# One head of each of two batches changes its layout, and five queues get a new order: fused clustered attention and gated MLP

## The chip, the cores and the metric

One core of a Trainium2 chip. The metric is the device time of one execution of the kernel in microseconds; the median of several runs counts. The profiled execution is one more run, with its own time.

## What is computed

Four batches of eight heads of attention over 768 positions with 64 numbers per head. Each query and each key is given to one of 16 clusters (the nearest centroid by cosine), and a query sees only keys of its own cluster. The output, 512 wide, goes through a gated MLP that also mixes positions.

```python
mask = q_assign[:, :, :, None] == k_assign[:, :, None, :]
scores = scale * np.matmul(q, k.transpose(0, 1, 3, 2))
scores = np.where(mask, scores, -1000000000.0)
scores = scores - np.max(scores, axis=-1, keepdims=True)
attn = np.exp(scores)
attn = attn / (np.sum(attn, axis=-1, keepdims=True) + 1e-09)
x = np.matmul(attn, v)                      # per head; heads side by side: B x 768 x 512
...
h = np.maximum(x @ w_in, 0.0)
u, v = (h[..., :d_ff // 2], h[..., d_ff // 2:])
v_n = (v - mu) / np.sqrt(var + 1e-06)
v_s = np.einsum('ts,bsd->btd', w_spatial, v_n) + b_spatial[None, :, None]
return (u * v_s) @ w_out
```

## The kernel before

The 32 heads are numbered batch by batch; two heads side by side are a pair (pair 9 is heads 18 and 19, pair 14 is heads 28 and 29), four pairs a batch. `prep(n)` loads a pair (raw, vraw), splits it into f16 parts (hq, lo, vhl), finds the clusters (logits on TensorE, L733 to L735) and appends them as one-hot rows to the operands. `attend(n)` does the attention of a pair, six tiles of 128 rows per head, and transposes the pair's result into the MLP's input (L988). `mlp(b)` does a batch's MLP in tiles: v (L1007), u and s (L1067), p (L1007).

A head is laid out in one of two ways, and the set `ROW` says which.

- In `ROW`, queries lie on partitions. A tile is a score pass (L912, L914: four matmuls), a row maximum on VectorE (L917) with two small operations (L918, L919), the exponential on ScalarE (L920), a cast to f16 (L922), a subtraction on GpSimd that makes the low part (L923), a transpose of both parts by DMA (L928, p<-pt, issued by SyncE), and a value pass of 18 matmuls (L932) that reads what was transposed.
- Not in `ROW`, keys lie on partitions, and nothing is transposed: score pass (L948, L950), exponential (L954), cast (L956), subtraction (L957), value pass (L962). But the maxima of the queries must be known beforehand: `shifts` makes nine passes of maxima (L851 on TensorE, L858 on VectorE), reduces them (L870), writes three columns (L871, L874), transposes them by DMA (L892) and copies the rows into the operand (L893). Where one head of a pair is of this kind, `prep` also makes the mean of the pair's values (L807 to L820).

```python
rowed = 2 * n in ROW and 2 * n + 1 in ROW
...
if 2 * n + h in ROW:
    continue                                    # shifts: no maxima
...
for k in range(NT if 2 * n + h in ROW else 0):  # attend: queries on partitions
...
for k in range(0 if 2 * n + h in ROW else NT):  # attend: keys on partitions
```

The code records operations; nothing is issued while it runs. `Plan.run` then issues them engine by engine in the order that the table `ORDER` gives: for TensorE, ScalarE, VectorE, GpSimd and SyncE one list of numbers each, in which a number is the place of an operation among its engine's in the code. Every queue works strictly in that order, and an instruction that waits holds up all behind it on its queue. Nearly all DMAs, the transposes among them, stand in SyncE's queue. The wide matmuls of the MLP of one batch stand in TensorE's list between the passes of the next batch's heads. In the beginning there are 76 matmuls of ones that only keep TensorE busy (L558).

Of the kernel before, what the change touches and what calls it, by code (L numbers as in the profile page):

```python
# [129 lines left out]
ROW = (11, 13, 15, 17, 19, 20, 21, 22, 23, 24, 25, 26, 27, 28, 29, 30, 31)  # L130
# [23 lines left out]
""",  # L154
    "ACT": """
# [15 lines left out]
""",  # L171
    "DVE": """
# [1031 lines left out]
```

## Time and profile before

| | us |
|---|---|
| median of 3 runs | 619.76 (619.69 to 622.02) |
| the profiled execution | 619.86 |
| its span, from the first to the last instruction | 618.1 |
| TensorE busy, matmuls | 596.0 (96%) |
| ScalarE, VectorE, GpSimd busy | 455.7, 444.7, 421.7 |

Busy times are those in which an engine has an instruction under way; a busy TensorE is not one at its peak. The share of the DMA engines counts packets that overlap, so that it goes above 1. The granted clock is TensorE's, as a share of 2.4 GHz.

### The profile page before, as it was taken

The numbers are of one execution on the slowest core, as the hardware profiler recorded it, in microseconds if no ns is written. First come the engines' busy times: TensorE is split into PE (matmuls) and PEld (weight loads), VectorE is DVE, ScalarE is ACT, GpSimd is POOL, SyncE is SP. The second block draws the span as 40 slices with busy tenths as digits, with TensorE's granted clock in tenths as the row PEclk, the third lists the DMA queues.
The fourth block names the chain that finished last, engine by engine and source line by source line (L and its number), as shares of the span: only waits on it lengthen the run. The fifth ranks groups of instructions, "written<-read, shape, count | busy, mean of one in ns | idle before, by whom it ended". The sixth has DMA issues, their size and how long they took to land.

```text
span 618.1 us, 16885 instructions
## 1 busy us (share of the span) xinstructions
PE 596.0 (96%) x6779; PEld 379.3 (61%) x6779; DVE 444.7 (72%) x974; ACT 455.7 (74%) x706; POOL 421.7 (68%) x305
## 2 busy tenths in 40 slices
PE   8999998989999999999999999999899999999997
PEld 4566666756655577676565668755455578544564
DVE  6999999989998897688786777966486675142210
ACT  5699998999867698888988968777687886223112
POOL 2387898899775779698978777766488778133120
PEclk9999999999999999999999999999899999999999
DMA  6576588685588799999999999999999999600002
GB/s 217 143 179 145 154 153 159 145 197 127 168 177 172 197 180 188 189 217 193 216 194 188 193 199 221 215 181 183 192 206 207 193 184 203 128 17 18 18 17 103
DMA packets 226236, 101.59 MB, mean 164 GB/s; under 512 B 210791, under 2 KB 212654, under 8 KB 226158
## 3 DMA queue, kind: packets, MB, share of 16 engines
q1 hardware_dynamic: 222414, 94.02, 78.8%
q10 hardware_dynamic: 3744, 6.49, 2.9%
q8 instruction: 53, 0.87, 0.6%
q14 instruction: 25, 0.20, 0.1%
HBM read 27.63 MB, written 6.29 MB: 55 GB/s over the span
## 4 chain that ended last, share of the span: by engine, by line
PE 68%; DVE 14%; DMA 7%; ACT 5%; issue 3%; POOL 1%; SPq 1%; ACTq 0%; DVEq 0%; POOLq 0%
PE acc L1067 21%; PE acc L1007 17%; PE acc L932 7%; DMA p<-pt 5%; PE sc L912 4%; PE sc L914 4%; PE acc L962 4%; DVE nm L858 4%; PE sc L948 3%; PE sc L950 3%; PE acc L851 3%; ACT p L920 2%; DVE rs L917 1%; DVE lo L702 1%; DMA sht<-shx 1%
## 5 line engine op out<-in xcount | busy, mean ns | idle before, releaser
L923 POOL TENSOR_TENSOR pt<-p,pt 128x768 f16<-128x768 f32 x102 | 169.3, 1670 | 57.9 <-ACT pt L922 22.9
L957 POOL TENSOR_TENSOR pt<-p,pt 128x768 f16<-128x768 f32 x90 | 149.8, 1687 | 30.2 <-ACT pt L956 24.6
L920 ACT ACTIVATE p<-sc,rs 128x768 f32<-128x768 f32 x102 | 100.7, 990 | 51.5 <-DVE rs L919 24.3
L917 DVE TENSOR_REDUCE rs<-sc 128x1 f32<-128x768 f32 x102 | 96.8, 953 | 57.6 <-PE sc L914 51.5
L1067 PE MATMUL acc<-wsp,vn 128*128 128x512 f16 (+1 forms) x576 | 101.3, 326 | 0.0
L858 DVE TENSOR_REDUCE nm<-acc 128x1 f32<-128x512 f32 (+1 forms) x135 | 86.8, 680 | 6.3 <-PE acc L851 6.0
L922 ACT CAST pt<-p 128x768 f16<-128x768 f32 x102 | 83.5, 829 | 4.3 <-DMA p<-pt 2.3
L932 PEld LDWEIGHTS <-p 128*128 128x128 f16 x1836 | 66.5, 97 | 20.3 <-DMA p<-pt 6.9
L954 ACT ACTIVATE p<-sc 128x768 f32<-128x768 f32 x90 | 71.9, 810 | 7.6 <-PE sc L950 3.4
L1067 PEld LDWEIGHTS <-vn 128*128 128x128 f16 x576 | 54.8, 98 | 33.0
L932 PE MATMUL acc<-vhl,p 128*128 128x65 f16 (+1 forms) x1836 | 69.7, 193 | 5.5 <-DMA p<-pt 3.5
L956 ACT CAST pt<-p 128x768 f16<-128x768 f32 x90 | 73.0, 832 | 0.4
L1067 PE MATMUL acc<-xT,win 128*128 128x256 f16 (+1 forms) x384 | 68.8, 326 | 0.0
L1007 PE MATMUL acc<-win,xT 128*128 128x512 f16 x288 | 67.4, 379 | 0.0
L1007 PE MATMUL acc<-wou,ghl 128*128 128x512 f16 x264 | 62.7, 383 | 0.4 <-ACT v L1023 0.4
L962 PEld LDWEIGHTS <-pt 128*128 128x128 f16 x1620 | 57.5, 97 | 8.5 <-issue 1.3
L962 PE MATMUL acc<-vhl,pt 128*128 128x65 f16 (+1 forms) x1620 | 61.4, 193 | 0.0
L912 PE MATMUL sc<-lo,hq 128*128 128x512 f16 x204 | 50.1, 327 | 1.3 <-ACT p L920 1.2
L1067 PEld LDWEIGHTS <-win 128*128 128x128 f16 x384 | 36.7, 97 | 23.5
L914 PE MATMUL sc<-hq 80*128 80x512 f16 x204 | 50.3, 327 | 0.0
L851 PE MATMUL acc<-hq 80*128 80x512 f16 (+1 forms) x180 | 46.7, 325 | 2.0 <-DVE nm L858 1.4
L948 PE MATMUL sc<-hq,lo 128*128 128x512 f16 (+1 forms) x180 | 43.9, 325 | 2.4 <-ACT p L954 1.4
(135 smaller groups left out, 929.0 us busy)
## 6 DMA issues: line engine op xcount, KB each, us to landing
raw<-in_kqT_dram SPq DMA_DIRECT2D x15, 768.0 KB
vraw<-in_vp_dram SPq DMA_DIRECT2D x16, 384.0 KB
out_dram<-wraw ACTq DMA_DIRECT2D x24, 256.0 KB
hq<-hq SPq DMA_DIRECT2D x15, 384.0 KB
hq<-lo SPq DMA_DIRECT2D x16, 192.0 KB
lo<-hq SPq DMA_DIRECT2D x16, 192.0 KB
wraw<-in_wsT_dram SPq DMA_DIRECT2D x6, 384.0 KB
vn<-in_w_in_dram SPq DMA_DIRECT2D x4, 512.0 KB
```

Of the source, the lines that this page charges most:

```text
L858: V.tensor_reduce(out=nm.t[:, t, k:k + 1] if n == 1 else nm.t[:, t:t + n, k], in_=src, axis=AX.X, op=ALU.max, negate=True)
L912: T.matmul(out=sc.t[:, cs], lhsT=hq.t[:, 2, h, ks], rhs=lo.t[:, h, cs], start=True, stop=False)
L914: T.matmul(out=sc.t[:, cs], lhsT=hq.t[0:R_SH, 1, h, ks], rhs=hq.t[0:R_SH, 0, h, cs], start=False, stop=True)
L917: o = op("DVE", 0.95, lambda sc=sc, rs=rs: V.tensor_reduce(out=rs.t[:, 0:1], in_=sc.t[:, 0:S], axis=AX.X, op=ALU.max, negate=True), after= ...
L920: o = op("ACT", 0.99, lambda sc=sc, p32=p32, rs=rs: A.activation(out=p32.t, in_=sc.t[:, 0:S], func=AF.Exp, bias=rs.t[:, 2:3], scale=rs.t[: ...
L922: o = op("ACT", 0.83, lambda pt=pt, p32=p32: A.copy(out=pt.t[:, 0, :], in_=p32.t), after=[o], use=[p32], new=[pt], key=K_HI)
L923: o = op("POOL", 1.65, lambda pt=pt, p32=p32: G_.tensor_tensor(out=pt.t[:, 1, :], in0=p32.t, in1=pt.t[:, 0, :], op=ALU.subtract), after=[o ...
L932: T.matmul(out=av.t[:, k * (D + 1):k * (D + 1) + w], lhsT=rt()[:, c, :], rhs=rhs, skip_group_check=True, **f)
L957: o = op("POOL", 1.65, lambda pt=pt, p32=p32: G_.tensor_tensor(out=pt.t[:, 1, :], in0=p32.t, in1=pt.t[:, 0, :], op=ALU.subtract), after=[o ...
L962: T.matmul(out=av.t[:, t * (D + 1):t * (D + 1) + w], lhsT=lhsT, rhs=rhs, skip_group_check=True, **f)
L1007: T.matmul(out=acc.t, lhsT=lr[m][0], rhs=lr[m][1], start=(m == 0), stop=(m == n - 1))
L1067: T.matmul(out=o.rearrange("p (t q) -> p t q", q=P), lhsT=lr[m][0], rhs=lr[m][1], start=(m == 0), stop=(m == total - 1), skip_group_check= ...
```

## The change

Head 18 goes into `ROW` and head 28 out of it. Both heads of pair 9 are then in `ROW`, so that pair 9 needs no mean of values; pair 14 needs one. All five lists of `ORDER` are replaced; no other line is touched. Of the lists the diff shows one line each way.

```diff
-ROW = (11, 13, 15, 17, 19, 20, 21, 22, 23, 24, 25, 26, 27, 28, 29, 30, 31)
+ROW = (11, 13, 15, 17, 18, 19, 20, 21, 22, 23, 24, 25, 26, 27, 29, 30, 31)
...
-839 836 837 831 827 825 828 840 826 841 842 829 830 832 845 843 844 846
+835 829 825 836 826 840 841 827 837 828 842 830 831 832 845 843 844 846
...
```

SyncE's queue behind the transposes of head 17, first before and then after. A row with L928 is the transpose of one tile; its number is the buffer's.

Before, from the pair copies to the first four tiles of head 19:

```order
L781 DMA lo<-hq 64x1536
L780 DMA hq<-oht 16x768
L988 DMA_TRANSPOSE xT_105<-xhl 128x12x128
L690 DMA vraw<-in_vp_dram 128x768
L928 DMA_TRANSPOSE p_5635<-pt 128x12x128
L928 DMA_TRANSPOSE p_5701<-pt 128x12x128
L708 DMA hq<-hq 64x2x1536
L777 DMA_TRANSPOSE oht<-ohx 128x6x128
L689 DMA raw<-in_kqT_dram 128x1536
L928 DMA_TRANSPOSE p_5729<-pt 128x12x128
L780 DMA hq<-oht 32x768
L928 DMA_TRANSPOSE p_5744<-pt 128x12x128
```

The six tiles of head 17 stand ahead of these rows, with nine other DMAs behind the last of them; no tile of head 18 is transposed. After, from the fourth tile of head 17 to the fifth of head 18:

```order
L928 DMA_TRANSPOSE p_5179<-pt 128x12x128
L780 DMA hq<-oht 32x768
L928 DMA_TRANSPOSE p_5272<-pt 128x12x128
L928 DMA_TRANSPOSE p_5314<-pt 128x12x128
L928 DMA_TRANSPOSE p_5386<-pt 128x12x128
L710 DMA hq<-lo 64x1536
L928 DMA_TRANSPOSE p_5353<-pt 128x12x128
L928 DMA_TRANSPOSE p_5458<-pt 128x12x128
L780 DMA hq<-oht 16x768
L690 DMA vraw<-in_vp_dram 128x768
L928 DMA_TRANSPOSE p_5509<-pt 128x12x128
L928 DMA_TRANSPOSE p_5588<-pt 128x12x128
```

Three tiles of head 17 (5179, 5272, 5314) are followed at once by tiles of head 18 (its second, 5386, ahead of its first, 5353).

SyncE's queue at head 27, where in the order after the one transpose of head 28's maxima stands (L892) and the copy of its rows (L893):

```order
L928 DMA_TRANSPOSE p_7940<-pt 128x12x128
L781 DMA lo<-hq 64x1536
L928 DMA_TRANSPOSE p_7976<-pt 128x12x128
L928 DMA_TRANSPOSE p_8031<-pt 128x12x128
L892 DMA_TRANSPOSE sht<-shx_84 128x6x128
L928 DMA_TRANSPOSE p_8088<-pt 128x12x128
L893 DMA hq<-sht 3x768
```

Before, the queue has neither row there; the six tiles of head 28 follow those of head 27.

VectorE's queue in the order after, with head 28's passes of maxima (L858, into nm) between the row operations of other heads (L917 to L919):

```order
L919 TENSOR_SCALAR rs<-rs 128x1
L858 TENSOR_REDUCE nm_89<-acc_115 128x1
L917 TENSOR_REDUCE rs<-sc_111 128x1
L858 TENSOR_REDUCE nm_89<-acc_115 128x2
L858 TENSOR_REDUCE nm_89<-acc_113 128x1
L918 TENSOR_SCALAR rs<-rs 128x1
L858 TENSOR_REDUCE nm_89<-acc_115 128x1
L858 TENSOR_REDUCE nm_89<-acc_113 128x2
L858 TENSOR_REDUCE nm_89<-acc_115 128x1
L919 TENSOR_SCALAR rs<-rs 128x1
```

Before, the last passes of maxima in this queue are head 18's.

## Rows read from the trace of the kernel before

**Rows 1.** Engines by stretch: us from:to, length, each one's busy time, clock, DMA share.
```profile
0.00:140.00 140.00, 129.72 (x1783) 86.76 (x1784) 130.39 (x278) 122.53 (x217) 104.94 (x84) 1.00 0.71 165
140.00:205.00 65.00, 64.08 (x706) 38.21 (x705) 59.50 (x120) 53.37 (x89) 48.03 (x33) 1.00 0.67 159
205.00:292.20 87.20, 86.30 (x1083) 58.90 (x1082) 69.26 (x142) 71.62 (x109) 70.44 (x47) 1.00 1.03 197
292.20:327.00 34.80, 34.80 (x453) 22.03 (x451) 27.41 (x66) 30.31 (x45) 30.58 (x23) 1.00 1.00 204
327.00:405.00 78.00, 76.72 (x951) 52.58 (x948) 58.54 (x134) 62.80 (x85) 59.70 (x41) 1.00 1.14 199
405.00:441.00 36.00, 32.15 (x336) 18.28 (x334) 21.67 (x55) 26.25 (x36) 22.04 (x16) 0.95 1.12 196
...
sum 618.10, PE 595.96 PEld 379.32 DVE 444.71 ACT 455.68 POOL 421.70; mean PE 59.60 PEld 37.93 DVE 44.47 ACT 45.57 POOL 42.17
```

The columns are PE, PEld, DVE, ACT, POOL (with their instructions), clock, DMA share, GB/s.

**Rows 2.** TensorE's waits, 285 to 470 us: total, times, longest.
```profile
PE acc L932 <- DMA p<-pt: 3.5, 3, 2.3
```

**Rows 3.** Issues of L928 on SyncE, 205 to 327 and 327 to 441 us: ns shortest/median/longest.
```profile
L928 SPq DMA_TRANSPOSE p<-pt x25: 1295/1493/3443, 215.2 to 326.9; - x25
...
L928 SPq DMA_TRANSPOSE p<-pt x39: 1430/1857/3902, 329.7 to 439.5; - x39
```

**Rows 4.** The chain that ended last, in order of time: start, us, what.
```profile
275.52 5.72 DMA p<-pt
...
428.64 7.26 DMA p<-pt
```

**Rows 5.** TensorE's instructions around 289 to 294 us: start, us, what.
```profile
289.60 1.46 PE L1007 MATMUL acc<-wou,ghl 128*128 128x512 f16 x6
290.89 0.49 PE L948 MATMUL sc<-hq,lo 128*128 128x512 f16 x2
...
291.55 0.49 PE L948 MATMUL sc<-hq,lo 128*128 128x512 f16 x2
...
292.20 0.71 PE L932 MATMUL acc<-vhl,p 128*128 128x65 f16 x18
292.75 0.18 PE L733 MATMUL acc<-cmh,hq 128*128 128x32 f16 x1
...
293.65 0.70 PE L932 MATMUL acc<-vhl,p 128*128 128x65 f16 x18
```

**Rows 6.** TensorE's instructions, 434 to 452 us; in brackets idle time before, and releaser.
```profile
435.95 0.78 PE L932 MATMUL acc<-vhl,p 128*128 128x65 f16 x18 [2.33 <-DMA p<-pt]
...
437.80 2.49 PE L1007 MATMUL acc<-wou,ghl 128*128 128x512 f16 x6
440.13 0.71 PE L932 MATMUL acc<-vhl,p 128*128 128x65 f16 x18
...
451.96 0.38 PE L912 MATMUL sc<-lo,hq 128*128 128x512 f16 x1 [1.03 <-ACT p L920]
```

**Rows 7.** SyncE's issues at head 17's fourth tile and head 26's first.
```profile
285.09 6.60 SPq L928 DMA_TRANSPOSE p<-pt x3
...
431.40 2.52 SPq L928 DMA_TRANSPOSE p<-pt  x1
```

**Rows 8.** Groups of instructions by line: busy us, mean ns of one, idle before.
```profile
L923 POOL TENSOR_TENSOR pt<-p,pt 128x768 f16<-128x768 f32 x102 | 169.3, 1670 | 57.9 <-ACT pt L922 22.9 <-issue 17.8 <-POOL pt L923 5.3
...
L920 ACT ACTIVATE p<-sc,rs 128x768 f32<-128x768 f32 x102 | 100.7, 990 | 51.5 <-DVE rs L919 24.3 <-PE acc L932 13.1 <-PE acc L1007 3.6
L917 DVE TENSOR_REDUCE rs<-sc 128x1 f32<-128x768 f32 x102 | 96.8, 953 | 57.6 <-PE sc L914 51.5 <-ACT pt L922 3.1 <-ACT vn L1042 1.7
L858 DVE TENSOR_REDUCE nm<-acc 128x1 f32<-128x512 f32 (+1 forms) x135 | 86.8, 680 | 6.3 <-PE acc L851 6.0
L922 ACT CAST pt<-p 128x768 f16<-128x768 f32 x102 | 83.5, 829 | 4.3 <-DMA p<-pt 2.3 <-DMA lo<-hq 0.6 <-PE acc L962 0.3
...
L954 ACT ACTIVATE p<-sc 128x768 f32<-128x768 f32 x90 | 71.9, 810 | 7.6 <-PE sc L950 3.4 <-POOL pt L957 3.0 <-issue 0.8
```

130 rows, old and new, of the table ORDER are left out of this document.

## The prediction

> **What bounds the kernel now.** I read the busy time of each engine in stretches first, then TensorE's waits, then the issues of SyncE's queue, then the chain that ended last, and last TensorE's instructions one by one. TensorE is busy for 595.96 of 618.10 us [rows 1], so at most 22.1 us of idle time can be won. The stretches say where it lies. Up to 140 us VectorE is the full engine (130.39 of 140.00) and TensorE idles 10.3 us; from 140 to 405 us TensorE idles only 3.1 us of 265; from 405 to 441 us it idles 3.85 us, and the granted clock falls to 0.95. The profiled execution took 619.86 us, 1.76 more than its span; the median of the three runs, 619.76, is 0.1 below it. About 0.5% (3.1 us) is what a measurement of this kernel can tell from no change.
>
> The idle time at 405 to 441 us has one cause. TensorE's waits between 285 and 470 us are led by the value pass (L932) that waits for a tile's transpose, p<-pt: 3.5 us in three waits, the longest 2.3 [rows 2]. The chain shows that one: a transpose issued at 428.64 lands 7.26 us later [rows 4], and the value pass starts at 435.95 after 2.33 us of idling [rows 6]. Behind it six 512-column matmuls take 2.33 us (437.80 to 440.13) where the same six took 1.29 us at 289.60 [rows 5, 6]: TensorE is at the lower of its two levels, 1.2 GHz, after the wait. So this late transpose cost itself and some 1.7 us more (1.04 on these six, the rest on the passes ahead of them).
>
> Transposes are late there because the queue that carries them is full. The 25 issued between 215 and 327 us hold SyncE for 1493 ns in the middle case, near the shortest (1295); the 39 between 330 and 440 us for 1857 ns [rows 3]. The DMA share says the same: 1.03 and 1.00 ahead of 327 us, 1.14 and 1.12 behind it [rows 1]. The share counts overlapping packets; I take 1.14 as full, and so what lacks from it as idle time of the DMA engines: 0.14 of 1.14, 4.3 us, in the 34.8 us ahead of 327, and 0.11 of 1.14, 8.4 us, in the 87.2 us ahead of those.
>
> **The change, part by part.** *Sums on the engines.* Head 18 loses nine passes of maxima on VectorE (9 x 0.68 = 6.1 us, L858) and gains six row maxima (6 x 0.953 = 5.7 us, L917, with two small operations each); its six exponentials go from 810 to 990 ns, 1.1 us more on ScalarE [rows 8]. Head 28 does the reverse, and the mean of values moves from pair 9 to pair 14. Over the kernel these cancel: zero. Moved forward by five pairs, they add under 2 us to VectorE, which is busy for 27.41 of 34.80 us there [rows 1]: covered.
>
> *TensorE.* The same instructions in both orders: zero. What counts is how much of its work stands between the same two points. From the fourth value pass of head 17 (before, at 292.20 us) to the first of head 26 (440.13) I count in the order before 51 score passes, 51 value passes, 57 groups of six wide matmuls and 5 of logits; after 51, 51, 58 and 4. By their starts a score pass takes 0.66 us (290.89 to 291.55), a value pass 0.55 (292.20 to 292.75), six matmuls 1.29 and the logits of a pair 0.90 [rows 5]: 139.9 us before (0.2 for head 18's pass of means among it), 140.2 after. Equal. The trace took 147.9 us for it, so 8 us went to waits and to the lower clock.
>
> *The queue of transposes.* Here the change has its price. Between the same two points 45 tile transposes are issued before and 51 after: the six of head 18 come in, and nothing that head 18 needed before is as long. One load of raw (768 KB) leaves this part; it now stands ahead of it. Before, the part took from 285.09 us (the first issue of the three) to 431.40, 146.3 us [rows 7]. At the 199 GB/s of the full stretch [rows 1] a tile's 128 x 1536 x 2 bytes, 393 KB, take 2.0 us and the load 3.9. So 6 x 2.0 - 3.9 = 8.1 us are added to a queue that has some 5.0 us of idle time in its first 42 us to take them (the 4.3 us, and a tenth of the 7 us ahead of 292.2). 146.3 - 5.0 + 8.1 = 149.4 us, against 147.9 that TensorE spent: **+1.5 us**. Bounds: if none of the idle time is used, +6.5 us. If the transposes also start early enough to use the 8.4 us before 292 us, the queue would need 141.0 us, about TensorE's own 140.2, and every wait of this part goes: -6.9 us, and no less, since TensorE's work remains. I take the middle value, since the idle share of 292 to 327 us lies inside the part and that of the stretch before only touches it.
>
> The Trainium skill, page "DMA: Bandwidth & Descriptors", section "Latency and other measured facts", gives a DMA transpose 261 GB/s when its middle dimension is not contiguous. By that figure a tile would take 1.5 us (an estimate from that page), six 9.0, and the sum would be -1.5 instead of +1.5; the 199 GB/s that this trace moved with 39 transposes in flight speak against it.
>
> *Head 17's first tile.* In the order after, 11.4 us of TensorE's work stand between its scores and its values, 17.3 before (by the same durations). Its path is row maximum 0.95, two small operations, exponential 0.99, cast 0.83, subtraction 1.67 [rows 8], then the transpose; the one of this tile took 5.72 us to land [rows 4]. Together 10.2 us and the small operations: it just fits. Bounds 0 and +2.5 us if one other pass of 0.8 to 1.7 us gets between on ScalarE or GpSimd; I take 0. If it is late, what follows in the queue is late with it.
>
> *Head 28.* Nine maxima, a transpose and a row copy now come before its scores. Between its landing and those scores lies as much work as for the other transposes around it, so it has no wait of its own unless the queue lags. In exchange, behind head 27 the queue has six transposes less to carry. Before, that part waits little (1.03 us at 451.96, for an exponential [rows 6]): 0, bounds -1.0 and +1.0.
>
> *The first 140 us.* Everything is ordered anew, but no instruction leaves, and VectorE is full: 0, bounds -2 and +2 us (a fifth of the 10.3 us idle there).
>
> Sum: 619.86 + 1.5 = 621.4; against the median, 0.1 lower: **621.3 us**.
>
> **The rivals.**
> 1. *The idle DMA time is not filled* (slower). Head 18's transposes stand behind head 17's in one queue, so if head 17's are late the engines idle as before and the whole lag shows: +6.5, with one more fall of the clock (1.7) and without the relief of an earlier start: 619.8 + 6.5 = 626.3, 628 with the clock. For it: the share was 1.00 there with transposes ready to go; head 17's first tile has 6 us less cover. Against: six more tiles stand ready behind it. It decides when the part's queue needs over 152 us.
> 2. *The lag never builds up* (faster). The queue starts full early enough, and the 3.5 us of waits for p<-pt, the 1.7 us of slow clock and the smaller waits go: 619.8 - 6.9 = 612.9. For it: the DMA share before 285 us leaves 8.4 us. Against: transposes before 285 us depend on TensorE's scores, and those are not earlier.
> 3. *The first 140 us decide.* The new order there fits VectorE better or worse by 2 us; with +1.5 from above unchanged this is 619 to 623.
>
> That the change does not do what it says is excluded: the order shows head 18's six transposes and head 28's nine maxima.
>
> **How the numbers follow.** Forecast 0.42 (its own range 618 to 624), rival 1 0.25, rival 2 0.23, rival 3 0.10. The range takes in the forecast, rival 3, most of rival 1 and half of rival 2: 614.5 to 627. Faster by over 0.5% is below 616.7: rival 2, and 0.01 of the rest, 0.24. Slower is above 622.9: rival 1, and 0.06 from the upper end of the forecast, 0.31. Within 0.5%: 0.45.
>
> **What would show it.** Right: the DMA share of the 35 us before head 17's last value passes rises from 1.00 to 1.1; the value passes of heads 18 to 26 show some 8 to 10 us of waits for p<-pt and of slow clock; after head 27 hardly any wait for it is left. The forecast is wrong if TensorE's waits for p<-pt vanish and its clock stays at 2.4 GHz from 285 us on (rival 2), if they exceed 13 us (rival 1), or if the idle time before 140 us differs from 10.3 us by more than 2 us, which would put the difference where I put nothing.

## The result, and the profile after

| | before | after |
|---|---|---|
| median of 4 runs | 619.73 us (619.69 to 622.02) | 629.63 us (626.20 to 630.77) |
| ratio | | 1.0131, interval 1.0094 to 1.0169 |
| the profiled execution, its span | 619.86, 618.1 | 626.20, 624.4 |

The change makes the kernel 1.3% slower, above the range. The profiled execution is the shortest of its four, so the profile shows 6.3 us and the median 9.9: the other 3.6 us have to be looked for where this profile doesn't show them. The ratios here and below leave out executions that took over 1.5% more than the shortest of the same kernel; the profiled ones of two kernels below, of 637.83 and 631.15 us, are among these.

The engines by stretch, the kernel after (columns as in [rows 1]):

```profile
0.00:140.00 140.00, 129.70 (x1777) 86.04 (x1778) 129.10 (x278) 122.06 (x218) 106.68 (x83) 1.00 0.70 167
...
292.20:327.00 34.80, 31.56 (x372) 18.93 (x370) 26.37 (x67) 28.12 (x41) 27.09 (x20) 1.00 1.06 197
327.00:405.00 78.00, 74.96 (x906) 49.97 (x906) 57.15 (x134) 61.68 (x83) 56.37 (x40) 1.00 1.13 196
405.00:441.00 36.00, 31.39 (x309) 17.96 (x310) 22.54 (x53) 23.96 (x34) 18.49 (x14) 1.00 1.09 208
...
293.44:328.24 34.80, 32.16 (x389) 19.61 (x390) 26.71 (x70) 29.33 (x43) 26.98 (x20) 1.00 1.10 206
```

The first 140 us are as before in this execution (129.70 us busy, 129.72 before). From 292 to 441 us TensorE idles 10.9 us (3.24 + 3.04 + 4.61) where it idled 5.1; the clock stays at 1.00, so the 1.7 us that the lower level cost before are not there. The DMA share at 292 to 327 us went from 1.00 to 1.06. The same piece of work begins 1.24 us later here (293.44 instead of 292.20); counted from there, in the last row, the share is 1.10.

TensorE's waits between 285 and 470 us, the kernel after:

```profile
PE acc L932 <- DMA p<-pt: 6.6, 9, 1.4
PE sc L912 <- ACT p L920: 3.6, 2, 2.9
```

Against [rows 2], the waits for a transpose went from 3.5 us in three to 6.6 in nine. And there is a new one: a score pass that waits 2.9 us for an exponential. Where that comes from, TensorE's and ScalarE's instructions and SyncE's issues around 437 us show (one fence each; idle time and releaser in brackets; the first row is where the stretch used below begins):

```profile
293.44 0.33 PE L932 MATMUL acc<-vhl,p 128*128 128x65 f16 x5 [0.67 <-DMA p<-pt]
...
440.26 0.48 PE L912 MATMUL sc<-lo,hq 128*128 128x512 f16 x2 [2.92 <-ACT p L920]
...
446.80 0.38 PE L932 MATMUL acc<-vhl,p 128*128 128x65 f16 x7
```

```profile
434.75 0.82 ACT L922 CAST pt<-p 128x768 f16<-128x768 f32 x1
438.78 0.34 ACTq L1131 DMA_DIRECT2D out_dram<-wraw  x1
439.22 0.99 ACT L920 ACTIVATE p<-sc,rs 128x768 f32<-128x768 f32 x1 [3.64 <-DMA p<-pt]
```

```profile
433.65 5.11 DMA p<-pt
```

ScalarE is done with its cast at 435.57 and does nothing until 438.78. What stands next in its queue is an output DMA (L1131) that has its data. It is issued 0.02 us after the transpose of head 25's fifth tile lands (433.65 + 5.11 = 438.76). All DMAs of SyncE and ScalarE signal on the same eight semaphores, and in the trace's semaphore events this output DMA and that transpose have the same one; the program lets it wait until the earlier user is done. The exponential behind it is late by 3.2 us for a transpose that it doesn't need. In the kernel before, the same output DMA (the second tile of batch 1) is issued at 430.20 us while a cast runs, and holds nothing up.

For what follows I use one length that runs of any start can be compared by: **the stretch** from the fourth value pass of head 17 to the first of head 26. Before it is 440.13 - 292.20 = 147.9 us [rows 5, 6]; after, with the starts 293.44 and 446.80, 153.4. Of the 6.4 us by which TensorE's last matmul moved, 5.4 lie in the stretch, 1.2 ahead of it, and -0.3 behind it; from 446 to 540 us no wait of TensorE's is left.

The prediction's sum was about another length, the part of SyncE's queue from the issue of head 17's fourth tile to that of head 26's first, 285.09 to 431.40 before. After, these are issued at 285.48 and 440.14 us. The two parts, before and after:

```profile
285.09:431.40 146.31, 143.11 (x1751) 93.44 (x1748) 108.56 (x254) 121.58 (x169) 112.08 (x78) 1.00 1.10 199
```

```profile
285.48:440.14 154.66, 143.89 (x1678) 90.69 (x1677) 111.55 (x270) 118.71 (x163) 108.41 (x76) 1.00 1.12 199
```

The queue's part takes 154.7 us, 8.3 more, at the same 199 GB/s. TensorE's stretch grew by less, since a tile's value pass now follows its transpose more closely: at head 26 it began 8.7 us behind the issue before (440.13 - 431.40) and begins 6.7 behind it after (446.80 - 440.14).

### The profile page after: what moved, and what is told of

Same layout as the page of the kernel before. It is cut to its first block, busy times and chain, and to the rows that moved or that the text cites. A ratio compares the mean times of both kernels' runs of the same rounds, so it can differ in the third digit from the quotient of the medians.

```text
span 624.4 us, 16885 instructions
## 1 busy us (share of the span) xinstructions
PE 597.3 (96%) x6779; PEld 377.5 (60%) x6779; DVE 439.7 (70%) x974; ACT 456.7 (73%) x706; POOL 421.9 (68%) x305
## 4 chain that ended last, share of the span: by engine, by line
PE 59%; DVE 13%; DMA 11%; ACT 7%; issue 5%; POOL 3%; SPq 2%; ACTq 0%; DVEq 0%; POOLq 0%
PE acc L1067 19%; PE acc L1007 12%; DMA p<-pt 8%; PE acc L932 6%; PE acc L962 5%; DVE nm L858 4%; PE sc L912 3%; PE sc L914 3%; PE acc L851 3%; PE sc L948 2%; PE sc L950 2%; ACT p L920 2%; POOL pt L923 2%; DVE lo L702 1%; DVE rs L917 1%
## 5 line engine op out<-in xcount | busy, mean ns | idle before, releaser
L917 DVE TENSOR_REDUCE rs<-sc 128x1 f32<-128x768 f32 x102 | 97.1, 954 | 66.1 <-PE sc L914 55.1
L858 DVE TENSOR_REDUCE nm<-acc 128x1 f32<-128x512 f32 (+1 forms) x135 | 87.3, 682 | 6.1 <-PE acc L851 5.3
L851 PE MATMUL acc<-hq 80*128 80x512 f16 (+1 forms) x180 | 47.0, 325 | 2.0 <-DVE nm L858 1.4
L1105 POOL TENSOR_TENSOR ghl<-u,ghl 128x512 f16<-128x512 f32 x22 | 26.1, 1190 | 33.5 <-issue 19.5
```

Of the source, the lines that this page charges most:

```text
L858: V.tensor_reduce(out=nm.t[:, t, k:k + 1] if n == 1 else nm.t[:, t:t + n, k], in_=src, axis=AX.X, op=ALU.max, negate=True)
L917: o = op("DVE", 0.95, lambda sc=sc, rs=rs: V.tensor_reduce(out=rs.t[:, 0:1], in_=sc.t[:, 0:S], axis=AX.X, op=ALU.max, negate=True), after= ...
```

## The experiments

Ratios are to the kernel before, with the 95% interval; the changed kernel has 1.0131. "As after" is the changed kernel.

**Half the bytes of head 18's transposes.** As after, with (m is 6 for head 18 and 12 for the others)

```diff
-nc.sync.dma_start_transpose(rt(), pt.t.rearrange("p a s -> p (a s)"))
+nc.sync.dma_start_transpose(rt()[:, 0:m, :], pt.t.rearrange("p a s -> p (a s)")[:, 0:m * P])
-lhsT=rt()[:, c, :]
+lhsT=rt()[:, c % NT if 2 * n + h == 18 else c, :]
```

> The changed kernel; the six transposes of head 18 carry only the first half of their bytes (196 KB instead of 393), and its value passes read that half twice, so the low part of head 18's weights is left out. TensorE's matmuls, the order and all other work are as in the changed kernel. Theory V (volume: the queue of transposes is the limit between about 285 and 440 us, and what head 18 adds to it is added to the time): 6 x 1.0 = 6 us less in the queue, so 4 to 6 us less time than the 626 to 631 of the changed kernel, and the waits of value passes for p<-pt (6.8 us) fall to about 2. Theory O (order: the loss comes from single places where the new order makes one thing late, the mean of pair 8 and an exponential at 436 us): less than 1.5 us, and the waits at these two places stay.

Measured: 1.0087 (1.0059 to 1.0115); the stretch takes 149.96 us, 3.4 less; the waits for p<-pt in the whole kernel fall from 6.8 us to 3.1. Volume counts in the stretch. In the time it is 0.44% (2.7 us), less than expected, and the interval overlaps that of the changed kernel. The waits at the two places of theory O stayed (1.4 and 2.7 us): both theories hold a part.

**One head of the two at a time.** The lists of ORDER are put together from both kernels, cut at head 24.

First both in ROW, with the order after and then that of before:

```diff
-ROW = (11, 13, 15, 17, 18, 19, 20, 21, 22, 23, 24, 25, 26, 27, 29, 30, 31)
+ROW = (11, 13, 15, 17, 18, 19, 20, 21, 22, 23, 24, 25, 26, 27, 28, 29, 30, 31)
```

> Half of the change: head 18 queries on partitions, and head 28 stays so too. The five queues follow the changed kernel's order up to the first tiles of head 24 and the order of before from there. Theory V: head 18 alone is the cost, so 625 to 629, that is 5 to 9 us above before; head 28's six transposes come at 465 to 490 us, where the queue no longer limits, and cost under 1 us. Theory H28 (the loss comes from head 28's passes of maxima and the order behind head 24): within 2 us of before, 618 to 622.

Measured: 1.0115 (1.0079 to 1.0151), stretch 150.03 us. Head 18 alone makes the kernel slower. In this run the order of before stands behind head 24, and the output DMA shown above does not hold ScalarE up: it is issued at 442.46 us, during a cast. The stretch is 3.3 us shorter than the changed kernel's with the same 51 transposes. But behind the stretch TensorE needs 176.9 us instead of 174.0 (174.3 before), with 2.2 us of waits for p<-pt where the changed kernel has none: head 28's transposes cost more there than the 1 us expected.

Then neither in ROW, with the order of before and then that after:

```diff
-ROW = (11, 13, 15, 17, 18, 19, 20, 21, 22, 23, 24, 25, 26, 27, 29, 30, 31)
+ROW = (11, 13, 15, 17, 19, 20, 21, 22, 23, 24, 25, 26, 27, 29, 30, 31)
```

> The other half of the change: head 28 keys on partitions with its pass of maxima, and head 18 stays so too. The five queues follow the order of before up to the last tiles of head 24 and the changed kernel's from there. Theory V: within 2 us of before, 618 to 622, the 3.5 us of waits for p<-pt in front of head 26 unchanged. Theory H28: 624 to 628.

Measured: 0.9962 (0.9934 to 0.9991), stretch 145.37 us. The half with head 28 is a small gain; not as expected, since the waits for p<-pt fell from 3.5 to 1.0 us. 2.6 us of it lie in the stretch, ahead of head 26. In this order the output DMA holds up ScalarE for 1.6 us too.

**The mean's copy earlier in SyncE's queue.** As after, with one row of SyncE's list moved up by five rows (seven, says the expectation):

```diff
 L819 DMA mean<-wh
+L820 DMA mean<-wl
...
-L820 DMA mean<-wl
 L777 DMA_TRANSPOSE oht<-ohx
```

> The changed kernel with one row of SyncE's queue moved: the second copy of pair 8's mean of values (L820) stands right behind the first (L819), seven rows earlier. TensorE's 1.5 us wait for it at 268.5 us should go in any case. Theory V: the queue that limits from 285 us on gains nothing by that, so the time stays within 0.7 us of the changed kernel; the 1.5 us come back as longer waits for p<-pt. Theory O: 1.5 to 2 us less.

Measured: 1.0132 (1.0100 to 1.0165). The wait is gone. TensorE's row of the mean in the changed kernel; in this one it has no wait:

```profile
270.01 0.36 PE L962 MATMUL acc<-mean,hq 83*128 83x65 f16 x6 [1.54 <-DMA mean<-wl]
```

The stretch is 152.82 us, 0.5 less, and the time is the same: this wait was worth nothing that can be told.

**The output DMA in SyncE's queue.** As after, with

```diff
-op("ACT", 0.06, lambda: A.dma_start(out=out[b, t * P:(t + 1) * P, :], in_=o32()), ...
+op("SP" if (b, t) in OUT_SP else "ACT", 0.06, lambda: (nc.sync if (b, t) in OUT_SP else A).dma_start(out=out[b, t * P:(t + 1) * P, :], in_=o32()), ...
```

where OUT_SP is (1, 1): the second tile of batch 1 alone.

> The changed kernel with one DMA moved to another queue: the output of the second tile of batch 1 (L1131), which stands in ScalarE's queue and is issued there 0.02 us after the transpose of head 25's fifth tile lands at 438.76, ScalarE being idle for 3.2 us before it, stands in SyncE's queue behind the first transpose of head 26. Theory S (ScalarE's queue is held up by this DMA, which waits for a transpose that has nothing to do with it, since both signal on the same semaphore; the late exponential behind it costs the 2.9 us that TensorE waits at 437.3): the time between the fourth value pass of head 17 and the first of head 26 falls from 153.4 to about 150.5, and the total by 2 to 3 us. Theory V (only the volume of the queue counts): the 2.9 us come back as waits for p<-pt, within 1 us of the changed kernel.

Measured: 1.0091 (1.0059 to 1.0122), stretch 149.35 us, 4.0 less. TensorE's waits in it:

```profile
PE acc L932 <- DMA p<-pt: 6.2, 7, 1.6
...
PE sc L912 <- ACT p L920: 0.8, 2, 0.7
```

The 2.9 us for the exponential are gone and have not come back as waits for transposes: theory S holds for the stretch. In all six profiles that have head 18 in ROW and this part of the order, with the DMA in ScalarE's queue, ScalarE idles 3.0 to 3.6 us in front of it. The time falls by 0.4%, but the interval overlaps that of the changed kernel.

> Both edits together: head 18's transposes carry half their bytes (the low part of its weights is left out), and the output DMA stands in SyncE's queue. If the loss is the sum of the two, volume (3.4 us measured for half the bytes) and the held-up ScalarE (2.9), the same stretch takes 147 us, as before the change (147.9), and the total is within 1.5 us of before. If one only hides the other, it stays at 149.5 to 150.5.

Measured: 1.0055 (1.0023 to 1.0088), stretch 147.05 us. In the stretch the two nearly add up: 6.3 us less than after, where each alone took off 3.4 and 4.0, and it is as long as before. The total is not: 0.55% are left, and they lie elsewhere.

> Heads 18 and 28 both with keys on partitions (six transposes less than before), with the output DMA in SyncE's queue, since ScalarE was idle for 1.6 us in front of it there too. Theory S: 1 to 1.6 us less than the same kernel with the DMA in ScalarE's queue, 0.4 to 0.8% faster than before. Theory V: as that kernel, 0.3 to 0.4% faster than before.

Measured: 0.9963 (0.9937 to 0.9988), stretch 144.97 us against 145.37. Moving the DMA gains nothing that can be told here. Neither head in ROW is the shortest kernel of the study (median 619.13 us, before beside it 622.12), by less than the 0.5% that I took for the least that can be told.

**More volume in the kernel before.** Before, with

```diff
+    def spare(head):
+        if head == 19:
+            nc.sync.dma_start(out=out[3].rearrange("(p r) d -> p (r d)", p=P)[:, 0:S], in_=bbc)
-nc.sync.dma_start_transpose(rt(), ...)
+spare(2 * n + h) or nc.sync.dma_start_transpose(rt(), ...)
```

> The kernel before, its order and layout unchanged, with six more DMAs of 393 KB (a constant written to a part of the output that the last batch overwrites), one ahead of each transpose of head 19. This adds to the queue what head 18's six transposes would, and nothing to any engine. Theory V: half a microsecond of time for each microsecond of queue as in the halved case, so 4 to 7 us for 8 to 12 us of transfers, most of it as waits of value passes for p<-pt between 310 and 440 us. If volume is not the cause: under 2 us.

Measured: 1.0096 (1.0061 to 1.0132), some 6 us; TensorE's waits for p<-pt between 285 and 470 us are 6.1 us in six, as after the change (6.6), and the stretch is 150.3, 2.4 more than before. With no other order and no other layout, more transfers in the queue bring these waits. They are plain writes, not transposes (240 GB/s were moved at 292 to 327 us). Of the 4.5 us by which TensorE's last matmul moved in this profile, 2.2 lie behind the stretch, and the profile is the shortest of its six runs: the 6 us are not all explained.

**A twelfth of the bytes.** As the halved case with the DMA moved, with m = 1 and block 0 read twelve times.

> The changed kernel with the output DMA in SyncE's queue, and the six transposes of head 18 carrying a twelfth of their bytes; its value passes read that one block twelve times, so nearly all of head 18's weights are left out. With half the bytes this kernel is 0.55% above before. If the cost of volume goes on in a straight line: 0.2% or less above before, and the stretch from the fourth value pass of head 17 to the first of head 26 takes 144 to 145 us. If the queue no longer limits with half the bytes: 0.4 to 0.6% above before, 146.5 to 147.5 us.

Measured: 1.0067 (1.0046 to 1.0088), stretch 147.30 us. No gain over half the bytes: about half of head 18's transposes, 6 us, cost TensorE nothing. The other half, 6 us too, lengthens the stretch from 147.05 to 149.35 us (3.4 us where the output DMA stands in ScalarE's queue), so part of it is hidden as well.

**The first 140 us.** The remaining half per cent had to be ahead of the stretch. The profiles of the edited kernels with the new order came to the first score pass of head 10 (146.6 us after, 146.0 before) at 147.5, 151.6, 151.9, 156.8 and 159.0. So the early orders were exchanged, cut at about 140 us.

First the kernel before with the new order up to there; the edit is in the five lists of ORDER alone.

```diff
-ORDER: before
+ORDER: after up to 140 us, then before
```

> The kernel before, its layout and its order from about 140 us on, but the five queues follow the changed kernel's order up to there. Theory E: 2 to 3 us slower than before (0.3 to 0.5%), with a wider spread from run to run, and nothing changed behind 146 us. Otherwise within 0.2% of before.

Measured: 1.0054 (1.0030 to 1.0079). Theory E holds; the stretch (146.17 us) is not longer than before.

Then the changed kernel with the order of before up to there, without and with the output DMA moved.

```diff
-ORDER: after
+ORDER: before up to 140 us, then after
```

> The changed kernel's layout and its order from about 140 us on, but the five queues follow the order of before up to there. Theory E (part of the loss lies in the first 140 us: there the new order more often lets a VectorE instruction wait for GpSimd, as in the profiles of four edited kernels that reached 146 us some 5 to 13 us later than the two shown): 2 to 3 us less than the changed kernel, 0.8 to 1.0% above before. If the first 140 us cost the same in either order: as the changed kernel, 1.2 to 1.4% above before.

Measured: 1.0180 (1.0141 to 1.0219), and the stretch, too, is longer (155.9 us). 

> As the kernel with the order of before up to 140 us, and with the output DMA of batch 1's second tile in SyncE's queue instead of ScalarE's. Only the volume of head 18's transposes is then left of the three costs: 0.4 to 0.6% above before (2.5 to 3.5 us) if the three add up.

Measured: 1.0121 (1.0085 to 1.0158), stretch 150.2. Both miss, and as sums they speak against theory E. But a cut makes waits of its own (behind it TensorE waits 2.0 us for L618, and L790 and L702 take 1.98 and 2.20 us), and the first of the two loses 8.0 us in the stretch, where the early order does not reach. So I draw nothing from them on the first 140 us.

Where the time goes, two profiles with the same early order tell, one that came early and one that came late. VectorE's and GpSimd's instructions around 119 us, first the kernel after, then the one with the mean's copy moved:

```profile
118.91 0.94 DVE L790 SCALAR_TENSOR_TENSOR vhl<-vraw,vhl 128x768 f16<-128x768 f32 x1
...
121.29 1.82 DVE L702 SCALAR_TENSOR_TENSOR lo<-raw,hq 128x768 f16<-128x768 f32 x2
...
115.56 5.80 POOL L957 TENSOR_TENSOR pt<-p,pt 128x768 f16<-128x768 f32 x3
```

```profile
119.10 2.30 DVE L790 SCALAR_TENSOR_TENSOR vhl<-vraw,vhl 128x768 f16<-128x768 f32 x1
...
122.84 4.70 DVE L702 SCALAR_TENSOR_TENSOR lo<-raw,hq 128x768 f16<-128x768 f32 x2
...
115.73 4.85 POOL L957 TENSOR_TENSOR pt<-p,pt 128x768 f16<-128x768 f32 x3
122.78 6.27 POOL L957 TENSOR_TENSOR pt<-p,pt 128x768 f16<-128x768 f32 x3 [2.19 <-ACT pt L956]
```

The same instruction takes 0.94 or 2.30 us. In the first case GpSimd's three subtractions take 0.95 us longer (5.80 instead of 4.85): one of the two engines stands still while the other runs. In the second case L702 meets the next subtractions: 4.70 us for two instead of 1.82. VectorE, the full engine of these 140 us, loses 4.2 us.

The other profiles show the same. Eight begin with the changed kernel's order, and up to pair 3's L790 VectorE's rows lie within 0.6 us ahead of and 0.9 us behind the changed kernel's in all of them. From pair 4's L790 to the row behind L702 five lose 4.2 us each, and the other three nothing. In the five TensorE waits 2.4 us for L702 and 1.4 for L817 there, and its granted clock falls to 0.5 (1.2 GHz) for 3.4 us or more behind the one place or the other; in the three it falls nowhere before the last 5 us. The five come to head 10 at 150.8 us and later, the three by 147.7.

In the kernel with the output DMA moved, L790 of pair 3 waited as well, through the end of L986 and four subtractions:

```profile
90.88 7.46 DVE L790 SCALAR_TENSOR_TENSOR vhl<-vraw,vhl 128x768 f16<-128x768 f32 x1
```

```profile
90.22 0.91 POOL L986 TENSOR_TENSOR xhl<-xn,xhl 128x384 f16<-128x384 f32 x1
91.10 6.43 POOL L957 TENSOR_TENSOR pt<-p,pt 128x768 f16<-128x768 f32 x4
```

The Trainium skill, page "SBUF — State Buffer", section "SBUF: two separate sides", says that a VectorE instruction with two inputs in SBUF and one of GpSimd's that reads SBUF take the same port under an exclusive lock, which the one that starts first keeps for the whole instruction, the other being blocked. The rows agree on the lock: one runs at its full speed, and the other's time grows by about as long as it stands still (0.95 us, or 1.37 for the 1.49 that were left of the subtraction). They do not bear out that the row that begins first goes first: the subtraction's begins ahead of L790's in both cases, by 0.15 and 0.16 us, and in the first it was the subtraction that stood still.

**Without the VectorE instruction.** As after, with

```diff
-VL_POOL = (0, 1)
+VL_POOL = (0, 1, 3, 4)
```

> The changed kernel with the low part of the values of pairs 3 and 4 made by ScalarE and GpSimd (as in pairs 0 and 1 already) instead of VectorE's L790; ScalarE has two casts more (0.83 us each) and GpSimd two subtractions (1.7 us), VectorE two operations less. Theory P (the first 140 us lose time because VectorE stands still while GpSimd's subtractions run one after another): the profile comes to 146 us by 149 at the latest, and the kernel is 0.7 to 1.0% above before instead of 1.3. If VectorE's waiting for GpSimd is not what costs: the added work shows, 1.3 to 1.6% above before.

Measured: 1.0139 (1.0109 to 1.0169); the profile comes to head 10's first score pass at 149.0. A miss: no L790 of these pairs is left to wait, but the added work costs as much (waits of L851 for L858 3.4 us, 1.4 after), and L702 of pair 5 now waits (1.43 and 2.39 us). It settles nothing.

**The same row where GpSimd is idle.** As after, and as early_after, with one row of VectorE's list moved:

```diff
 L816 TENSOR_SCALAR wh_91<-acc_114 2x2x64
-L790 SCALAR_TENSOR_TENSOR vhl_87<-vraw,vhl_87 128x12x64
 L817 SCALAR_TENSOR_TENSOR ...
 L633 SCALAR_TENSOR_TENSOR acc_113<-wraw,acc_113 128x512
 L634 SCALAR_TENSOR_TENSOR acc_113<-wraw,acc_113 128x512
+L790 SCALAR_TENSOR_TENSOR vhl_87<-vraw,vhl_87 128x12x64
```

> The changed kernel with one row of VectorE's queue moved: L790 of pair 4 stands three rows later, behind L633 and L634, where GpSimd is idle for 1.2 us. Theory P (VectorE stands still while GpSimd works on, and this delay runs on through L702 and L817): the profile comes to 146 us by 148, and the kernel is 0.7 to 1.0% above before instead of 1.3. If something else delays the first 140 us: 1.2 to 1.4%.

Measured: 1.0081 (1.0052 to 1.0111); head 10's first score pass at 147.2; L790 takes its 0.95 us:

```profile
120.10 0.95 DVE L790 SCALAR_TENSOR_TENSOR vhl<-vraw,vhl 128x768 f16<-128x768 f32 x1
```

> The kernel before with the changed kernel's order up to 140 us, and in it the same row of VectorE's queue moved. Theory P: 0.0 to 0.3% above before instead of 0.54%. If something else delays the first 140 us: 0.4 to 0.6%.

Measured: 0.9998 (0.9972 to 1.0024). One row of one queue gives back the half per cent, in either kernel: 1.0131 to 1.0081, and 1.0054 to 0.9998; the intervals of the second pair do not meet. Theory P holds. In the profiles with the row moved L790 and L702 lose nothing. The last one still comes to head 10 at 149.5 us, 1.7 of it where VectorE waits for a load (L807).

**Both rows moved.**

> The changed kernel with both rows moved: L790 of pair 4 in VectorE's queue, and the output DMA of batch 1's second tile from ScalarE's queue to SyncE's. All of the computation is done. If the parts add up: 1.31 - 0.50 - 0.40 = 0.4% above before (0.2 to 0.6), and the stretch from the fourth value pass of head 17 to the first of head 26 takes 149 to 150.5 us. If they overlap: 0.7 to 0.9%.

Measured: 1.0070 (1.0046 to 1.0093), stretch 149.9 us. The stretch is as expected; the total is not: 0.7% is what the expectation gave for parts that overlap. Against the kernel with only L790 moved (1.0081, stretch 152.34) the DMA's move is worth 2.4 us of the stretch and 0.1% of the time, against the changed kernel 4.0 us and 0.4%. So of the three parts the lock is clear in the time (0.5%), while the held-up ScalarE (2.4 to 4.0 us) and half the volume (2.3 to 3.4 us) are clear in the stretch only, which varies by 1.0 us among kernels that differ in neither (152.34 to 153.36): in the time each is 0.1 to 0.4%, and the intervals overlap. Of the 5.0 us by which TensorE's last matmul comes later in this profile than before, 2.0 lie in the stretch, 2.4 ahead of it and 0.7 behind it. In those 2.4 VectorE waits 1.2 us for a load (L807); what makes the rest stays open.

## Why the prediction was wrong

**The queue of transposes: the number fits, the sum does not.** The forecast was 149.4 us, and with the output DMA out of ScalarE's queue the stretch takes 149.35 and 149.9. But 146.3 - 5.0 + 8.1 is a sum for SyncE's part of the queue, and I set it against 147.9, TensorE's stretch. The queue's part took 154.7 us, and 153.7 and 154.1 with the DMA moved: the 8.1 us came on top in full (146.3 + 8.1 = 154.4), and the 5.0 of idle time did not shorten it. TensorE's stretch is over 4 us shorter than that because its value passes follow the transposes more closely: with the DMA moved head 26's first comes 4.2 us behind the issue, 8.7 before. I had not worked that out, so the agreement is luck. What is right is the direction: the added bytes cost TensorE something, and only part of their 8.1 us. The DMA share rose to 1.10, as forecast. The 261 GB/s of the Trainium skill's page "DMA: Bandwidth & Descriptors" (section "Latency and other measured facts"), by which the sum would have been negative, did not show in this mix of transposes, loads and copies: 196 GB/s were moved at 327 to 405 us, 199 before.

**The step that failed first: "Over the kernel these cancel: zero".** I had summed ScalarE's instructions and not looked at what stands in its queue. Between two exponentials it has output DMAs, and one of them now waits for a transpose. It costs 153.4 - 149.4 = 4.0 us of the stretch, 2.4 in the kernel with the other row moved, more than the 1.5 of the whole forecast; in the time 0.1 to 0.4%, not clear of the spread.

**The step that failed second: "The first 140 us ... 0, bounds -2 and +2".** No instruction leaves, and VectorE is full, as I wrote. But an equal sum doesn't mean an equal time where two engines exclude each other. The new order puts L790 within 0.2 us of the start of a GpSimd subtraction, and a run loses 0 or 4.2 us there, by which goes first: L790 of pair 4 took 2.3 us in five of eight profiles of that order. Pair 3's took 7.5 in two of them, the executions of 637.83 and 631.15 us. Neither was longer than 1.23 in the six profiles that begin with the order of before. The profile of the change has neither wait; that the median has pair 4's shows in the 0.5% that moving L790 gives back. Rival 3 named the place, with half the price (2 us).

**Head 17's first tile, head 28.** The first fitted, as forecast: its transpose lands 1.9 us ahead of its value pass. Behind the first value pass of head 26 the changed kernel is 0.3 us faster, inside the bounds of 1; that the order from head 24 on, with head 28 out of ROW and head 18 left as it was, gains 0.4% I had not seen.

**Rival 1** gave a number close to the profile (626.3). Its sign came: the part's queue needed over 152 us (154.7). Its price did not: the whole lag was to show in TensorE as 6.5 us, and without the held-up ScalarE TensorE lost 1.4 to 2.0. The clock did not fall, and the waits for p<-pt were 6.6 us, not 13. So its number, too, was met by luck.

## What to carry to other kernels

In a program like this one, whose DMAs share a few semaphores, a DMA in the queue of a computing engine waits not only for its data, but also for the DMA that used its semaphore before; list these rows when another queue of transfers gets fuller. When a queue's length is worked out, set it against the same queue's length before, and ask by itself how far the engine follows behind it. Where VectorE is full, look up which of its two-input instructions stand next to runs of GpSimd's, and put them where GpSimd pauses. And where one profile stands for a kernel, compare it with the median first: here it was the shortest of four.

## What the runs showed of the hardware

Who goes next at the shared port cannot be read from the rows' starts. In six of the eight profiles of the new order pair 3's L790 began 0.67 to 0.70 us behind L986, and was done 1.03 to 1.05 us later, ahead of the next subtraction. In the other two it began 0.66 us behind it and waited through the rest of L986 and four subtractions that followed one another without a pause (6.6 us). Pair 4's L790 began 0.14 to 0.17 us behind its subtraction in all eight: at 0.14 it ran at once in one kernel (half the bytes) and waited in another (the kernel before with the new early order).
